# Row selection in attention plus mixture-of-depths: chosen rows fetched from DRAM instead of gathered by matmuls

## The chip, the cores and the metric

The kernel runs on one core of a Trainium2 chip. The metric is device time in microseconds (us) for one execution, the median of three runs. A profiled execution has its own time and, inside it, a span from the first to the last recorded instruction.

Engines are named as in the profile: PE (TensorE matmuls), PEld (its weight loads), DVE (VectorE), ACT (ScalarE), POOL (GpSimd), and SPq (SyncE's queue, which here only issues DMAs). Each engine runs its own instructions in program order, and waits between engines and DMAs go through semaphores that the framework places from the data dependences of the program as written.

## The reference

Inputs q, k, v have the shape (batch 8, heads 12, sequence 448, head size 64). The first half is cosine attention, the second a mixture-of-depths layer that changes only 128 chosen rows of each batch:

```
q_n = q / (norm(q) + 1e-6);  k_n = k / (norm(k) + 1e-6)
attn = softmax(q_n @ k_n^T / tau)
x    = (attn @ v) as (8, 448, 768)

scores = x @ w_gate
out    = x.copy()
for b in range(8):
    top = the 128 rows of batch b with the highest scores
    h   = relu(x[b, top] @ w1)                # 768 -> 1024
    g   = sigmoid(scores[b, top])
    out[b, top] = x[b, top] + g * (h @ w2)    # 1024 -> 768
```

## The kernel before

**Slots.** Two heads of one batch make a pair; there are N = 48 pairs, six to a batch (HP = 6). The main loop (L609) has one slot for each pair i: scores for pair i on PE, their exponentials on ACT, then the product with V for pair i-1 (`pv`, L309), its division into `x_tiles[b]` on DVE (`pv_evac`, L325), the transposes of q and k for pair i+1 (L251), and normalisation of pair i+2 on POOL (`scale`, L222). After `scale`, POOL converts V and (L349) the fresh 128 columns of x to bf16 (`half_x`, tile `xh`).

**Hooks.** The mixture-of-depths work of batch b is hung into later slots by a table: `at(slot, where, fn, ...)` appends a call to a list and `run(slot, where)` plays that list at a fixed place of the slot. The places, in program order within a slot, are D0 and D1 (early), P1b, then pv, A (right after pv_evac, before the slot's last scores), P2 (on POOL after `scale`, `values` and `half_x`), C, D3, and B (the slot's end). Calls at the same place run in the order in which they were appended. With s = 6(b+1), the first slot after batch b, the usual plan `late` (L531) is:

- store_x (L343) at s, place P2: two SPq DMAs that write the batch's x to `out`;
- gate at s+2 to s+5 (DVE); rank_prep at s+5 (POOL); rank_rep at s+5 B (PE); rank_count and pick at s+6 (DVE): `sel`, a one-hot 0/1 matrix of the chosen rows;
- select (L428) at s+7 A: eight small matmuls that give row indices and gate values, then DVE reductions; select_b on ACT;
- gather (L463) at s+7 B and s+8 A: 24 matmuls of `xh` against `sel` that give the chosen rows, already transposed, in PSUM; DVE copies them to `xeT`;
- ffn1 and ffn2 (L480, L509) in four parts at s+8 B to s+11 A: 48 and 16 matmuls;
- scatter (L514) at s+12 P2: an indirect DMA from POOL that adds the 128 result rows to those in `out` (compute_op=add).

The plans `mid`, `early` and `last` (L533 to L537) pull this forward for the last batches, so that two parts of ffn1 are evacuated by ACT there. All parts share the single PSUM bank `m_ps`.

**Order through DRAM.** scatter names the whole of `out_flat` as its target, since its rows are known only at run time. So a store_x later in the program waits for an earlier scatter to land, and a scatter waits for every earlier store.

**SPq** issues all loads of q, k and v (every third slot, L612, four groups ahead) and all stores, in program order.

**The end.** Batch 6 has its gather at slot 47 and its feed-forward after the loop. For batch 7, `gate` over the first 640 columns and four stores (two to `out`, two to a DRAM copy `x_copy`) stand at slot 47 P2; the last 128 columns (`x_last`) follow after the loop: two stores to `out`, two to `x_copy`. Then POOL issues scatter(6) (L704), an indirect fetch of batch 7's chosen rows from `x_copy` (L711), and, after two DVE operations that add them to the feed-forward result (L723), a plain last scatter (L726).

**Weights.** w1 and w2 are loaded with a cast by POOL at slots 7 and 10, P2 (L568, L569).

Of the kernel before, what the change touches and what calls it, by code (L numbers as in the profile page):

```python
# [17 lines left out]
def kernel(  # L18
# [18 lines left out]
    P = 128  # L37
# [115 lines left out]
    tokc = const.tile([P, NS, 2], BF16)  # L153
    for half in range(2):
        for col, base, step, mult in ((0, 0, 0, 4), (1, NC * half, 1, 3)):
            nc.gpsimd.iota(tokc[half * T:half * T + T, :, col], pattern=[[step, NS]],
                           base=base, channel_multiplier=mult,
                           allow_small_or_imprecise_dtypes=True)
# [150 lines left out]
    def pv(i):  # L309
        ex = exp_tiles[i]  # L310
        vo = vo_bufs[i % NB]
        for u in range(2):
            for j in range(NS):
                for c in range(NC):
                    nc.tensor.matmul(out=o_ps[:, u, j * E:(j + 1) * E],  # L315
                                     lhsT=ex[:, 2 * c + u, qc(j)],
                                     rhs=vo[:, u * NS + c], start=False,
                                     stop=(c == NC - 1), skip_group_check=True)
# [30 lines left out]
    def half_x(i):  # L349
        b, hp = divmod(i, HP)  # L350
        if hp == 0:
            xh_tiles[b] = xp.tile([P, NS, D], BF16, name="xh", bufs=3)
# [14 lines left out]
    def rank_prep(b, eng=nc.gpsimd):  # L367
        g = gates[b % 2]
        sg = moe.tile([P, NS, 3], BF16, name="sg")
# [58 lines left out]
    def select(b):  # L428
        sel, sg = st[b]["sel"], st[b]["sg"]
        pk = bank()  # L430
        for o, w, src in ((0, 2, tokc), (2, 3, sg)):
            for j in range(NS):
                nc.tensor.matmul(out=pk[:, o:o + w], lhsT=sel[:, j], rhs=src[:, j],
                                 start=(j == 0), stop=(j == NS - 1))
        gr = moe.tile([P, 1], FP32, name="gr")
        nc.vector.tensor_reduce(gr, pk[:, 2:5], axis=AX.X, op=ALU.add)  # L436
# [3 lines left out]
        nc.vector.tensor_scalar_add(idx, pks, float(b * S))  # L440
        st[b].update(idx=idx, gr=gr)
# [36 lines left out]


# [23 lines left out]

    def ffn2_evac(b, n, ps, eng):
        if n == 0:
            st[b]["oe"] = moe.tile([P, D], FP32, name="oe")
# [7 lines left out]
    def scatter(b):  # L514
# [3 lines left out]
            in_=st[b]["oe"][:CAP], in_offset=None, compute_op=ALU.add)  # L518
# [7 lines left out]
    def run(slot, where):  # L526
        for fn, args in work.pop((slot, where), []):
# [3 lines left out]
    late = dict(gate=((2, "D1"), (3, "D1"), (4, "D1"), (5, "D1")), rep=5, rank=6, select=7,  # L531
                ffn=((8, "B"), (9, "B"), (10, "B"), (11, "A")))
    mid = dict(late, ffn=((8, "B"), (9, "AA"), (9, "B"), (10, "A")))  # L533
    early = dict(gate=((2, "D1"), (3, "D1"), (3, "D1"), (4, "D1")), rep=4, rank=5,
                 select=6, ffn=((7, "B"), (8, "AA"), (8, "B"), (9, "A")))
    last = dict(gate=((1, "D1"), (2, "D1"), (2, "D1"), (3, "D1")), rep=3, rank=4,
                select=5, ffn=())  # L537
    for b in range(B - 1):
        s = HP * (b + 1)
        m = last if b == B - 2 else early if b == B - 3 else mid if b == B - 4 else late  # L540
        at(s, "P2", store_x, b)
        for j in range(NS):
            d, w = m["gate"][j]
            at(s + d, w, gate, b, j)
        at(s + m["gate"][3][0], "P1b", rank_prep, b)
        at(s + m["rep"], "B", rank_rep, b)
# [6 lines left out]
        at(s + m["select"], "B", gather, b, 0, "A" if b == B - 2 else "D")  # L553
        if b < B - 2:
            at(s + m["select"] + 1, "A", gather, b, 1)
        for (d, w), (fn, n) in zip(m["ffn"], ((ffn1, 0), (ffn1, 1), (ffn2, 0), (ffn2, 1))):
            at(s + d, w[0], fn, b, n, "A" if w == "AA" else "D")
            if fn is ffn2 and n == 1:
                at(s + d + 1, "P2", scatter, b)
    bb = B - 1  # L560
    gc = const.tile([P, NS], FP32)

    for j in range(NS):
        at(N - 1, "P2", gate, bb, j, 0, 5 * P, None, gc)
    at(N - 1, "P2", store_x, bb, None, 0, 5 * P)
    at(N - 1, "P2", store_x, bb, None, 0, 5 * P, x_copy)
    at(5, "D1", load_wg)
    at(7, "P2", load_w, w1_sb, moe_w1, kn[:, 1, 0, 0:1])  # L568
    at(10, "P2", load_w, w2_sb, moe_w2, kn[:, 1, 0, 0:1])  # L569
# [39 lines left out]
    for i in range(N + 1):  # L609
# [61 lines left out]
        if i < 3:  # L671
            warm(8)
        run(i, "B")
# [6 lines left out]
    pv_tails(N - 1)  # L680
    pv(N - 1)
    pv_evac(N - 1)
    gather(b, 1, "A", True)
    store_x(bb, x_last, 5 * P, D)
# [16 lines left out]
    for j in range(NS):  # L701
        rank_count(bb, j)
        pick(bb, j, nc.gpsimd if j < NC else nc.vector)
    scatter(b)  # L704
# [5 lines left out]
    xs = moe.tile([P, D], FP32, name="xs", bufs=1)  # L710
    nc.gpsimd.indirect_dma_start(  # L711
        out=xs[:CAP], out_offset=None, in_=x_copy[:, :],
        in_offset=bass.IndirectOffsetOnAxis(ap=st[bb]["row"][:CAP, 0:1], axis=0))
# [6 lines left out]
    oe = moe.tile([P, D], FP32, name="oe")  # L720
    for n in range(2):
        c = slice(n * ND, (n + 1) * ND)
        nc.vector.scalar_tensor_tensor(out=oe[:, c], in0=ps[n][:, :ND],  # L723
                                       scalar=st[bb]["gr"], in1=xs[:, c], op0=ALU.mult,
                                       op1=ALU.add)
    nc.gpsimd.indirect_dma_start(  # L726
        out=out_flat[:, :],
        out_offset=bass.IndirectOffsetOnAxis(ap=st[bb]["idx"][:CAP, 0:1], axis=0),
        in_=oe[:CAP], in_offset=None)
# [34 lines left out]
```

## Time and profile before

| what | value |
|---|---|
| median of three runs | 271.24 us (269.73 to 271.52) |
| profiled execution, its time | 268.42 us |
| its span | 266.6 us |
| around the span | 1.8 us |
| slots 17 to 34, mean length of six slots (one batch) | 29.1 us |
| end of the last scores to end of the span | about 28.5 us |

The slot lengths are read from the starts of the DVE copy qkT (L263), which occurs once in each slot. In the tables of the profile a group is a line of code, an engine and an operation, with its count, its busy time and the mean duration of one; "idle before" is the time that the engine stood still just ahead of it, with what ended that idle time. A DMA's "landing" runs from its issue to its completion, and its issuing instruction on POOL or SPq shows only the time to generate it. Busy time of PE counts overlapping matmuls, so its share is not a share of peak.

### The profile page before, as it was taken

What the parts mean: (1) busy time and instruction counts of PE and PEld (TensorE: products, weight loads), DVE (VectorE), ACT (ScalarE), POOL (GpSimd) and SP (SyncE); (2) the same over time, 40 slices, a digit from 0 to 9 for tenths busy, and PEclk for the clock granted to TensorE, in tenths of its full rate; (3) what the DMA queues carried; (4) which work ended last, traced back from release to release, by engine and by line L of the source; (5) the groups of instructions that cost most, each with busy time, mean ns of one, the idle gap of its engine ahead of it and who ended that gap; (6) DMA issues with size and microseconds to landing.
All of it is one profiled execution on the core that took longest, in us unless ns stands there. A gap on an engine that the chain in (4) does not pass through costs nothing.

```text
span 266.6 us, 10588 instructions
## 1 busy us (share of the span) xinstructions
PE 225.2 (84%) x4584; PEld 169.9 (64%) x4584; DVE 175.2 (66%) x472; ACT 203.3 (76%) x322; POOL 168.3 (63%) x234
## 2 busy tenths in 40 slices
PE   7678877586899979999899979998999899989920
PEld 6456655465678557767677757866786667757810
DVE  2424445474977778858877778678876976898401
ACT  3698999897897798888888789779878986683400
POOL 5367676979766568575966667757846885743131
PEclk9999999999999999999999999999999999999995
DMA  7999999999999974799679985999580049047861
GB/s 248 285 286 279 264 254 275 368 260 259 267 285 350 235 161 64 167 276 285 130 153 262 260 203 84 216 283 274 101 192 20 2 61 210 4 61 161 255 116 63
DMA packets 32431, 53.18 MB, mean 199 GB/s; under 512 B 2176, under 2 KB 28672, under 8 KB 31488
## 3 DMA queue, kind: packets, MB, share of 16 engines
q1 hardware_dynamic: 28976, 45.13, 63.9%
q0 software_dynamic: 2992, 6.69, 14.6%
q8 instruction: 36, 0.59, 1.0%
q10 hardware_dynamic: 416, 0.69, 0.7%
q14 instruction: 11, 0.09, 0.1%
HBM read 40.11 MB, written 15.53 MB: 209 GB/s over the span
## 4 chain that ended last, share of the span: by engine, by line
PE 35%; DMA 21%; DVE 16%; ACT 12%; issue 7%; SPq 4%; POOL 3%; POOLq 1%; ACTq 0%
DMA v_raw<-in_v_dram 11%; PE m_ps L491 7%; ACT expS L288 7%; PE m_ps L500 6%; PE sc L275 6%; PE o_ps L315 5%; DVE junk L416 4%; DVE junk L361 3%; DMA qk_raw<-in_k_dram 3%; DMA qk_raw<-in_q_dram 3%; PE sc L194 3%; ACT expS L291 3%; PE qkT_ps L257 3%; DVE xeT L457 2%; DVE x_b L333 2%
## 5 line engine op out<-in xcount | busy, mean ns | idle before, releaser
L288 ACT ACTIVATE expS<-sc 128x896 bf16<-128x896 f32 x144 | 125.3, 917 | 17.0 <-PE sc L275 16.4
L230 POOL TENSOR_TENSOR qkn<-qk_raw,rs 128x896 bf16<-128x896 f32 (+1 forms) x48 | 80.3, 1673 | 36.4 <-PE qkT_ps L257 26.3
L275 PE MATMUL sc<-qkT 64*128 64x448 bf16 x288 | 52.3, 358 | 14.8 <-DVE qkT L263 7.3
L187 ACT ACTIVATE sq<-qk_raw 128x896 bf16<-128x896 f32 x48 | 45.2, 947 | 2.1 <-DMA qk_raw<-in_k_dram 2.0
L315 PE MATMUL o_ps<-vo,expS 128*128 128x65 bf16 x1152 | 44.6, 193 | 1.5 <-issue 1.5
L315 PEld LDWEIGHTS <-expS 128*128 128x128 bf16 x1152 | 40.3, 97 | 2.1 <-issue 1.7
L275 PEld LDWEIGHTS <-qkT 64*128 64x128 bf16 x288 | 15.4, 92 | 37.3 <-issue 21.0
L263 DVE COPY qkT<-qkT_ps 128x960 bf16<-128x960 bf16 x48 | 31.3, 653 | 7.8 <-PE qkT_ps L257 6.8
L291 ACT ACTIVATE expS<-sc 128x448 bf16<-128x448 f32 x48 | 25.7, 536 | 13.3 <-PE sc L280 13.2
L333 DVE TENSOR_TENSOR x_b<-o_ps,rden 128x512 f32<-128x512 f32 x47 | 32.5, 691 | 1.6
L257 PEld LDWEIGHTS <-qkn 64*64 64x64 bf16 x1344 | 24.9, 109 | 12.9 <-issue 8.4
L257 PE MATMUL qkT_ps<-iden_b,qkn 64*64 64x64 bf16 x1344 | 30.4, 194 | 3.2 <-POOL qkn L230 2.1
L354 POOL CAST xh<-x_b 128x512 bf16<-128x512 f32 x47 | 29.7, 633 | 2.0 <-DVE gr L436 1.3
L361 DVE CUSTOM_DVE_ANT_0 junk<-x_b,wg_b 128x768 bf16<-128x768 f32 (+1 forms) x32 | 30.5, 953 | 0.5 <-DMA wg_b<-in_moe_w_gate_dram 0.3
L194 PE MATMUL sc<-sq,iden_b 128*128 128x112 bf16 x384 | 26.9, 215 | 2.4 <-ACT expS L288 2.3
L202 DVE TENSOR_REDUCE ss<-sc 128x14 f32<-128x112 f32 x48 | 12.8, 273 | 24.4 <-PE sc L194 24.0
L237 POOL CAST vo<-v_raw 128x448 bf16<-128x448 f32 x48 | 26.8, 557 | 0.8 <-DMA v_raw<-in_v_dram 0.7
L217 POOL TENSOR_SCALAR rs<-rs 128x28 f32<-128x28 f32 (+1 forms) x26 | 8.0, 307 | 25.8 <-ACT rs L211 21.7
L491 PEld LDWEIGHTS <-w_sb 128*128 128x128 bf16 x384 | 22.2, 98 | 3.3 <-issue 3.1
L194 PEld LDWEIGHTS <-iden_b 128*128 128x128 bf16 x384 | 20.8, 98 | 4.6 <-issue 1.7
L416 DVE SCALAR_TENSOR_TENSOR junk<-m_ps,own,tie 128x448 bf16<-128x448 f32 (+1 forms) x28 | 19.0, 678 | 0.5
L491 PE MATMUL m_ps<-xeT,w_sb 128*128 128x128 bf16 x288 | 18.1, 219 | 1.3 <-DVE xeT L457 1.3
(90 smaller groups left out, 275.6 us busy)
## 6 DMA issues: line engine op xcount, KB each, us to landing
qk_raw<-in_q_dram SPq DMA_DIRECT2D x15, 672.0 KB, 10.1
qk_raw<-in_k_dram SPq DMA_DIRECT2D x15, 672.0 KB, 12.0
v_raw<-in_v_dram SPq DMA_DIRECT2D x30, 192.0 KB, 9.6
out_dram<-x_b SPq DMA_DIRECT2D x7, 768.0 KB, 7.8
v_raw<-in_v_dram SPq DMA_DIRECT2D x30, 144.0 KB, 9.0
out_dram<-x_b SPq DMA_DIRECT2D x7, 576.0 KB, 4.7
w_sb<-in_moe_w_dram POOLq DMA_DIRECT2D x2, 1536.0 KB, 18.9
out_dram<-x_b SPq DMA_DIRECT2D x1, 640.0 KB, 6.7
```

The source lines that it names most:

```text
L187: nc.scalar.activation(sq_tiles[p], raw[gi % NRAW][0][:, :, g].rearrange("p a b d -> p a (b d)"), AF.Square)
L194: nc.tensor.matmul(out=dst, lhsT=iden_b, rhs=sq[:, :, s * D8:(s + 1) * D8], start=(s == 0), stop=(s == Dh // D8 - 1))
L230: eng.tensor_mul(kn[:, :, b0:b1], qk[:, :, g, b0:b1], rs[:, m, :, b0:b1].rearrange("p a (b o) -> p a b o", o=1) .to_broadcast([P, 2, b1 - ...
L257: nc.tensor.transpose(out=qkT_ps[r, o:o + T], in_=kn[r, a, s], identity=iden_b[r, r], tile_position=(u * T, u * T))
L263: nc.vector.tensor_copy(qkT_tiles[p], qkT_ps[:, :W])
L275: nc.tensor.matmul(out=sc[:, u, :S], lhsT=qkT[r, KO + c * P:KO + (c + 1) * P], rhs=qkT[r, :S], start=True, stop=True, tile_position=(u * D ...
L288: nc.scalar.activation(ex[:, 2 * c:2 * c + 2], sc[:, :, :S], AF.Exp, scale=inv_tau)
L291: nc.scalar.activation(ex[:, TAIL], sc[:, 0, :S], AF.Exp, scale=inv_tau)
L315: nc.tensor.matmul(out=o_ps[:, u, j * E:(j + 1) * E], lhsT=ex[:, 2 * c + u, qc(j)], rhs=vo[:, u * NS + c], start=False, stop=(c == NC - 1) ...
L333: nc.vector.tensor_mul(dst.rearrange("p j (u d) -> p j u d", u=2), o[:, :, :, :Dh], rden.to_broadcast([P, NS, 2, Dh]))
L361: nc.vector.tensor_tensor_reduce(out=junk[:, d0:d1], in0=src, in1=wg_b[:, d0:d1], scale=1.0, scalar=0.0 if prev is None else prev[:, j:j + 1],
L491: nc.tensor.matmul(out=ps[:, f * CAP:(f + 1) * CAP], lhsT=w1_sb[:, t, fc * P:(fc + 1) * P], rhs=xeT[t], start=(m == 0) if cut else (t == 0 ...
```

## The change

For batches 0 to 5 the rows are no longer gathered on PE. A new `fetch` reads the 128 chosen fp32 rows of x back from `out`, where store_x put them, by an indirect DMA from POOL; `half_xs` converts them to bf16 on POOL; `turn` transposes them by six PE transposes, and DVE copies the result. Those batches no longer convert x with `half_x`. The result is added to the fetched rows on DVE (in `ffn2_evac`, in place in `xs`), so their scatter is a plain write.

The places change too: store_x moves from s to s+3 for most batches, the fetch comes at the slot of select, half_xs one slot ahead of turn, and the four feed-forward parts move some slots later; ACT no longer evacuates any part inside the loop. The last batch's x is stored pair by pair at slots 43 to 47, to `x_copy` and to `out`. One of its four gate reductions is split into a POOL multiply and an ACT sum. The first part of the last pair's pv moves into slot 47. After the loop the fetch of batch 7 is issued ahead of scatter(6). In `select`, index and gate columns share one table `gtok`, so four matmuls do what eight did, and the index is reduced before the gate. The weight loads move to slots 8 and 14.

```diff
-    tokc = const.tile([P, NS, 2], BF16)
+    gtok = [const.tile([P, NS, 5], BF16, name=f"gtok{n}") for n in range(2)]
...
     def half_x(i):
         b, hp = divmod(i, HP)
+        if b < B - 2:
+            return
...
     def rank_prep(b, eng=nc.gpsimd):
-        sg = moe.tile([P, NS, 3], BF16, name="sg")
+        sg = gtok[b % 2][:, :, 2:]
...
     def select(b):
-        for o, w, src in ((0, 2, tokc), (2, 3, sg)):
-            for j in range(NS):
-                nc.tensor.matmul(out=pk[:, o:o + w], lhsT=sel[:, j], rhs=src[:, j],
-                                 start=(j == 0), stop=(j == NS - 1))
+        for j in range(NS):
+            nc.tensor.matmul(out=pk[:, :5], lhsT=sel[:, j], rhs=gtok[b % 2][:, j],
+                             start=(j == 0), stop=(j == NS - 1))
...
+    def fetch(b):
+        xs = moe.tile([P, D], FP32, name="xs")
+        st[b]["xs"] = xs
+        last = b == B - 1
+        nc.gpsimd.indirect_dma_start(
+            out=xs[:CAP], out_offset=None, in_=x_copy[:, :] if last else out_flat[:(b + 1) * S, :],
+            in_offset=bass.IndirectOffsetOnAxis(
+                ap=st[b]["row" if last else "idx"][:CAP, 0:1], axis=0))
+
+    def half_xs(b):
+        st[b]["xe"] = moe.tile([P, D], BF16, name="xe", bufs=1)
+        nc.gpsimd.tensor_copy(st[b]["xe"], st[b]["xs"])
+
+    def turn(b):
+        ps = bank().bitcast(BF16)
+        xe, xeT = st[b]["xe"], moe.tile([P, KD, CAP], BF16, name="xeT")
+        for t in range(KD):
+            nc.tensor.transpose(out=ps[:, t * CAP:(t + 1) * CAP],
+                                in_=xe[:, t * P:(t + 1) * P], identity=iden_b)
+        nc.vector.tensor_copy(xeT.rearrange("p t c -> p (t c)"), ps[:, :KD * CAP])
+        st[b]["xeT"] = [xeT[:, t] for t in range(KD)]
...
     def ffn2_evac(b, n, ps, eng):
+        if "xs" in st[b]:
+            c = slice(n * ND, (n + 1) * ND)
+            xs = st[b]["oe"] = st[b]["xs"]
+            nc.vector.scalar_tensor_tensor(
+                out=xs[:, c], in0=ps[:, :ND], scalar=st[b]["gr"], in1=xs[:, c],
+                op0=ALU.mult, op1=ALU.add)
+            return
...
     def scatter(b):
...
-            in_=st[b]["oe"][:CAP], in_offset=None, compute_op=ALU.add)
+            in_=st[b]["oe"][:CAP], in_offset=None,
+            **({} if "xs" in st[b] else dict(compute_op=ALU.add)))
...
+    late = dict(gate=(2, 3, 4, 5), rep=5, rank=6, select=7, turn=10, store=3,
+                ffn=("10B", "13B", "14B", "15A"))
+    plans = {b: late for b in range(B - 5)}
+    plans[B - 5] = dict(late, ffn=("10A", "12B", "13B", "14A"))
+    plans[B - 4] = dict(gate=(2, 3, 3, 4), rep=4, rank=5, select=6, turn=9, store=3,
+                        ffn=("9A", "11B", "12B", "13A"))
+    plans[B - 3] = dict(gate=(1, 2, 2, 3), rep=3, rank=4, select=5, turn=8, store=3,
+                        ffn=("8A", "8B", "9A", "11A"))
+    plans[B - 2] = dict(gate=(1, 2, 2, 3), rep=3, rank=4, select=5, store=0, ffn=())
...
+        if b == B - 2:
+            at(s + m["select"], "B", gather, b, 0, "A")
+        else:
+            at(s + m["select"], "P2", fetch, b)
+            at(s + m["turn"] - 1, "P2", half_xs, b)
+            at(s + m["turn"], "A", turn, b)
...
+    def gate_mul():
+        nc.gpsimd.tensor_mul(xg5, x_tiles[bb][:, NC, :5 * P], wg_b[:, :5 * P])
...
+    at(N - 1, "P2", gate_mul)
+    for hp in range(HP - 1):
+        for dst in (x_copy, None):
+            at(N - HP + 1 + hp, "P2", lambda d0=hp * P, dst=dst: store_x(
+                bb, x_tiles[bb][:, :, d0:d0 + P], d0, d0 + P, dst))
...
+            if fn is ffn2 and n == 1:
+                at(s + d + (place_ == "B"), "P2", scatter, b)
...
+        at(HP * (b + 1) + plans[b]["store"], "P2", store_x, b)
...
-    for j in range(NS):
+    for j in range(NC):
         at(N - 1, "P2", gate, bb, j, 0, 5 * P, None, gc)
-    at(N - 1, "P2", store_x, bb, None, 0, 5 * P)
-    at(N - 1, "P2", store_x, bb, None, 0, 5 * P, x_copy)
-    at(7, "P2", load_w, w1_sb, moe_w1, kn[:, 1, 0, 0:1])
-    at(10, "P2", load_w, w2_sb, moe_w2, kn[:, 1, 0, 0:1])
+    at(8, "P2", load_w, w1_sb, moe_w1, kn[:, 1, 0, 0:1])
+    at(14, "P2", load_w, w2_sb, moe_w2, kn[:, 1, 0, 0:1])
...
+        if not nxt:
+            pv_tails(i)
+            pv(i, (0,))
         run(i, "B")
...
-    pv_tails(N - 1)
-    pv(N - 1)
+    pv(N - 1, (1, 2))
     pv_evac(N - 1)
     gather(b, 1, "A", True)
+    xgs5 = moe.tile([P, 5 * P], FP32, name="xgs5", bufs=1)
+    nc.scalar.activation(xgs5, xg5, AF.Copy, accum_out=gc[:, NC:])
...
-    scatter(b)
     gather(bb, 0, "A", True)
...
+    fetch(bb)
+    scatter(b)
```

## The prediction

> **What bounds the kernel now.** I read the totals, then stretches of the loop, then the waits of the DMA queue, then the last 30 us in order of time. First the totals, and the busy time of one batch's 29 us, of the last slots and of the end:
>
> ```profile
> PE 225.2 (84%) x4584; PEld 169.9 (64%) x4584; DVE 175.2 (66%) x472; ACT 203.3 (76%) x322; POOL 168.3 (63%) x234
> ...
> 109.00:138.00 29.00, 27.42 (x575) 20.83 (x572) 22.17 (x58) 24.39 (x39) 20.38 (x28) 1.00 0.87 212
> ...
> 221.00:242.00 21.00, 19.86 (x390) 14.67 (x388) 18.08 (x48) 13.97 (x21) 10.13 (x15) 1.00 0.42 84
> 242.00:266.60 24.60, 12.44 (x145) 9.51 (x142) 7.64 (x26) 4.85 (x11) 6.71 (x11) 0.84 0.64 158
> ```
>
> Columns are length, PE, PEld, DVE, ACT and POOL busy, clock, DMA share, GB/s. In the middle PE is busy 27.4 of 29.0 us, ACT 24.4. PE sets the pace, and ACT is only 3 us below it: a slot relieved of PE work soon meets ACT. In the last 24.6 us PE is half idle, so a chain of waits rules there. The groups that the change touches:
>
> ```profile
> L473 PE MATMUL m_ps<-sel,xh 128*128 128x128 bf16 x160 | 11.1, 219 | 0.0
> L354 POOL CAST xh<-x_b 128x512 bf16<-128x512 f32 x47 | 29.7, 633 | 2.0 <-DVE gr L436 1.3 <-DVE x_b L333 0.8
> L457 DVE CAST xeT<-m_ps 128x512 bf16<-128x512 f32 x6 | 4.0, 672 | 0.0
> L457 DVE CAST xeT<-m_ps 128x256 bf16<-128x256 f32 x6 | 2.5, 412 | 0.0
> L515 POOL DMA_INDIRECT out_dram<-oe,idx x7 | 11.4, 1633 | 7.3 <-DMA x_copy<-x_last 6.3 <-issue 1.0
> ```
>
> Next SPq's own waits, then the end in order of time (start, duration):
>
> ```profile
> SPq L346 <- DMA out_dram<-oe,idx: 94.5, 6, 24.9
> ```
>
> ```profile
> 234.72 1.61 POOL L515 DMA_INDIRECT out_dram<-oe,idx  x1 [0.16 <-issue]
> ...
> 240.42 0.62 SPq L346 DMA_DIRECT2D out_dram<-x_b  x1
> ...
> 250.11 0.14 DVE L444 CAST row<-pks 128x1 int32<-128x1 f32 x1
> ...
> 253.78 1.60 POOL L515 DMA_INDIRECT out_dram<-oe,idx  x1 [6.30 <-DMA x_copy<-x_last]
> 256.14 1.02 POOL L711 DMA_INDIRECT xs<-x_copy,row  x1 [0.76 <-issue]
> 260.87 1.14 DVE L723 SCALAR_TENSOR_TENSOR oe<-w_ps,gr,xs 128x384 f32<-128x384 f32 x2 [7.65 <-DMA xs<-x_copy,row]
> 262.28 1.01 POOL L726 DMA_INDIRECT out_dram<-oe,idx  x1 [5.12 <-DVE oe L723]
> ```
>
> The reader should see two things. First, scatters and stores to `out` do wait for one another: scatter(5), issued at 234.72, lands 5.6 us later (the median for these), at 240.3, and the store behind it goes out at 240.42 although its x was ready at 237.5. Second, the row index of batch 7 is ready at 250.25, but its fetch goes out only at 256.14, because scatter(6) ahead of it on POOL waits for the last stores. PE has finished the last feed-forward at 255.1; the fetch lands at 260.7 and the rest follows.
>
> **What the Trainium skill says.** "DMA: Bandwidth & Descriptors", section "Two DMAs through the same engine are not ordered": the issuing engine has to wait for the first DMA's completion before a dependent one. The 94.5 us above are that wait. Section "Anatomy of one DMA — SWDGE (gpsimd) path" gives about 2.0 us plus bytes over 436 GB/s; for 128 rows of 3 KB my estimate from it is 2.9 us. This trace has 4.6 for the fetch and 5.6 for the adding scatter; I use the trace. "TensorE: Matmul & The Clock Gate", section "Part 4: PE-mode transpose", gives about 275 ns for a 128x128 bf16 transpose among other work. Here 28 transposes of 64x64 take 0.63 us together, so back to back they pipeline; the page's price is my upper bound only.
>
> **The body of the loop, batches 0 to 5.** PE loses the gather: 16 matmuls from 131.97 to 132.97 and 8 from 134.52 to 134.99, 1.47 us. It gains six transposes: at the gather's pace of 62 ns 0.37 us, at the page's price 1.65. I take 0.4. select drops four of eight matmuls that take 0.51 us in the chain, so 0.25. Net 1.3 us a batch, 7.9 us for six (0 at the page's price). What counts is what slots let through. The six slot lengths of a steady batch are 5.97, 4.70, 4.87, 4.77, 4.67, 4.28. The 4.28 slot carries 24 matmuls of ffn1 (1.5 us), so a slot with one ffn part costs about 4.4; the 5.97 slot carries both parts of ffn2. After: two slots with one ffn1 part each (4.4), one with both parts of ffn2 (5.97), one with rank_rep (4.7), one with select (4.87 - 0.25, led by DVE's rank_count), one with only turn (4.3, close to ACT's 4.1 a slot). Sum 28.4 against 29.3 (this batch, slots 18 to 23): **0.75 us a batch kept, 4.5 us in all** (ends 0 and 7.9).
>
> On other engines: DVE loses 0.67 + 0.41 and gains one copy of 768 bf16 columns, 0.53 at the pace of L263 (653 ns for 960); the new multiply-add takes 0.61 (L723) like the multiply before it. The two ffn1 evacuations taken from ACT (0.60 each) cost DVE 0.69 each, beside PE work. POOL loses 36 casts of 0.63 (22.8 us) and 0.6 a scatter (1.6 against 1.0 for the plain L726), and gains six fetches of 1.0 and six casts of 768 columns, 0.93 scaled from L354; POOL does not lead, so I count nothing. A fetch's 4.6 to 6 us are covered by the two slots (9.4 us) until half_xs. The 2.4 MB that the fetches read are 12 us of DMA at 200 GB/s, but the DMA share is 0.87; the loads run four groups ahead. Without that cover each fetch would add up to 2 us.
>
> Weights: w2's issue at slot 10 holds POOL (0.92 + 0.99) ahead of rank_prep(0), and PE stands 1.2 us for it (64.9). At slot 14 nothing so urgent is behind it: 0.5 us gained (0 to 1.2). First use of w2 is at slot 20, 27 us later, against 18.9 to land.
>
> store_x moves three slots towards the reuse of its x tile (two buffers): scatter(b-2) starts some 3.4 us after its slot's copy qkT, lands 5.0 later, then the second store 0.7 and its 7.8 us to land: 16.9. DVE overwrites the tile about 17.2 to 18 us after, and fetch comes at 21.9. I count 0, with 0.5 to 1 us of slack.
>
> **The end.** Late: ffn2's second part for batch 5 moves from slot 45 to 47, a swap within the PE-led slots. At slot 47 POOL now has gate_mul (1.28 us between 0.45 for 128 columns and 1.69 for 896), then scatter(5), **which stands in program order behind the pair store to `out` of that slot.** In before's time: x ready 237.5, four SPq issues of 0.62 to 240.2, landing 3.1 to 4.3 after the last one's start: 243.3. With 0.8 us of POOL's own latency scatter(5) runs 244.0 to 245.0. Behind it on POOL is xg (0.45), behind that on ACT the gate sum and the evacuation of ffn1(6), and PE's rank_rep_last waits for the gate. Before, these matmuls end at 244.6; now at 246.9, 2.3 later. (Slot 43 has the same wait for scatter(4), 1.5 to 2 us of POOL; the next transposes are just on time, so 0.) One gate reduction less on DVE (0.9) is offset by batch 5's multiply-add (0.61) in that slot.
>
> From there: row at 252.6; fetch at once, landed 257.3; PE done 257.4; multiply-adds 258.7; scatter(6), 1.8 after the fetch, lands 260.1; last scatter 260.3 instead of 262.28. **The end gains 2.0 us**: 6 from the early fetch, less 2.3 for the late row, less what scatter(6) takes. Ends: a loss of 1 if the store lands as slowly as the big ones (6.7), a gain of 5.3 if scatter(5) does not wait.
>
> **Sum**: 4.5 + 0.5 + 2.0 = 7.0 us off the profiled 268.42, so 261.4. The median of the runs is 271.24, 2.8 above the profiled run; the same difference gives **264.2 us**.
>
> **Rivals.** *No wait at slot 47* (chance 0.20): if the tracking does not tie scatter(5) to that store, the end gains 5.3: 260.9. Against it: the 2.9 us wait in the other direction at 240.42.
> *The gain is eaten by ACT and DVE* (0.20): ACT's 24.4 of 29 speaks for it, and qkT waits seen as idle PE; then the body keeps 0 to 1 and the end 2: 267 to 270.
> *The stores land late: slower* (0.14). From slot 21 on each store goes out right behind a scatter, and DVE's pv_evac in slot s+7, then POOL's fetch, wait for it; behind them are every later x_b, and POOL's `scale`. At 8.6 us of landing (7.8 plus slack) this starts to cost; stores here have taken up to 14.4 us. Three batches (2, 3, 4) pay: at 14.4 some 5.8 each, 17 in all less some slack, about 276. It ends slower than before by over 1% from 11.8 us of landing on (9.7 us over three batches). For it: the DMA share of 0.87 and new fetch traffic; against: all steady stores took 7.7 to 7.8.
> My forecast has 0.46.
>
> **How the numbers follow.** Within 1% of 271.24 (268.5 to 274.0) is about what cannot be told from no change. Faster: 0.44 + 0.20 + 0.09 = 0.73; same: 0.02 + 0.11 + 0.02 = 0.15; slower 0.12. Range 257.5 (no wait and most of the 7.9) to 270.5 (gain eaten).
>
> **What would show it.** Right: a steady batch of 28.3 to 28.7 us; x_b without a DMA wait; scatter(5) preceded on POOL by a wait of 3 to 5 us for the x_b store; the last fetch issued within 1 us of its row, and the last scatter bound by scatter(6) or PE. Wrong: DVE's x_b or POOL's fetch waiting on a store; xs late for half_xs; ACT's exponentials back to back with PE idle; transposes near 275 ns each.

## The result, and the profile after

The changed kernel is **slower**: 282.75 us (median, 280.56 to 286.86) against 271.38 for the kernel before, ratio 1.039 [1.030, 1.049]. Its profiled execution took 280.56 us with a span of 278.5 (before: 268.42 and 266.6). The forecast was 264.2. Runs of one kernel differ by up to 4%, so medians here are of all runs, ratios with their 95% intervals of the faster ones alone, within some 1.5% of the fastest, and a ratio is not the quotient of two medians.

First the totals, then busy time in two steady batches (slots 17 to 28) and in the last slots (length, PE, PEld, DVE, ACT, POOL busy, clock, DMA share, GB/s), all of the changed kernel but the line from 87.84, which is the same two batches in the kernel before:

```profile
PE 225.5 (81%) x4444; PEld 166.6 (60%) x4444; DVE 173.5 (62%) x466; ACT 204.0 (73%) x322; POOL 161.3 (58%) x215
...
89.59:148.11 58.52, 52.13 (x1080) 38.37 (x1078) 42.90 (x114) 48.30 (x77) 36.72 (x44) 0.99 0.76 198
...
87.84:145.51 57.67, 53.87 (x1122) 40.37 (x1122) 44.32 (x117) 48.57 (x78) 39.63 (x53) 1.00 0.81 189
...
225.00:256.00 31.00, 25.07 (x411) 17.15 (x410) 20.83 (x49) 14.97 (x22) 15.43 (x19) 0.83 0.38 103
```

No engine has noticeably more to do than before, and none is fuller. PE, busy 53.87 of 57.67 us (93%) in these slots before, is at 89%, and in the last slots at 81% with a clock of 0.83. So PE waits. The groups of the new operations, then the longest new waits (total, times, longest), the last line being ACT's wait before:

```profile
L494 POOL CAST xe<-xs 128x768 bf16<-128x768 f32 x6 | 7.9, 1311 | 2.7 <-DMA xs<-out_dram,idx 2.7
L500 PE MATMUL m_ps<-iden_b,xe 128*128 128x128 bf16 x36 | 3.7, 250 | 10.3 <-POOL xe L494 10.3
```

```profile
ACT expS L293 <- PE sc L282: 35.7, 21, 7.6
...
PEld L500 <- POOL xe L494: 11.1, 6, 3.0
...
ACT expS L291 <- PE sc L280: 13.2, 16, 1.5
```

Read the second group's last field: PE stood idle 10.3 us in all, always for the cast on POOL, in front of six sets of six transposes; a set costs 0.5 us. ACT's wait for the fourth block of scores, which PE computes right behind the transposes, was 13.2 us before and is 35.7 now.

The end in order of time. The forecast's sequence is there, late. The first line names a gate as what POOL waited for, but the scatter reads no gate, and the last pair store, issued at 252.37, landed at 254.8; so I read the 3.37 us as the wait for that store:

```profile
255.64 1.29 POOL L550 DMA_INDIRECT out_dram<-xs,idx  x1 [3.37 <-DVE gc L366]
258.01 0.45 POOL L746 TENSOR_TENSOR xg<-x_last,wg_b 128x128 f32<-128x128 f32 x1 [1.08 <-DVE x_last L336]
...
266.07 1.04 POOL L487 DMA_INDIRECT xs<-x_copy,row  x1 [3.07 <-DVE row L448]
267.41 1.64 POOL L550 DMA_INDIRECT out_dram<-oe,idx  x1 [0.30 <-ACT hT L465]
273.96 1.00 POOL L550 DMA_INDIRECT out_dram<-xs,idx  x1 [4.91 <-DMA out_dram<-oe,idx]
```

**Where the time went** is seen in the start of each slot's copy of qkT on DVE, one mark per slot (us from the start of the profiled execution). A slot's length is its mark less the one before. Transposes of fetched rows stand in slots 16, 22, 28, 34, 39 and 44. The lower rows are experiments told of below; that of "cast early" took 279.27 us, where the kernel's fastest run took 274.03.

| kernel | slot 16 | 28 | 32 | 35 | 39 | 44 | 46 | span |
|---|---|---|---|---|---|---|---|---|
| before | 87.84 | 145.51 | 166.11 | 181.03 | 200.25 | 224.92 | 233.81 | 266.6 |
| after | 89.59 | 148.11 | 166.96 | 184.31 | 207.23 | 237.60 | 246.38 | 278.5 |
| cast early | 89.29 | 148.69 | 167.48 | 185.98 | 208.60 | 237.15 | 246.09 | 277.5 |
| cast early, ffn1 at B | 90.99 | 151.57 | 169.71 | 186.23 | 206.31 | 233.01 | 244.02 | 274.1 |
| cast on ACT | 87.60 | 145.53 | 163.82 | 181.74 | 204.19 | 232.43 | 241.22 | 273.0 |
| transposes at slot end | 86.22 | 142.43 | 161.02 | 178.01 | 200.69 | 230.81 | 241.56 | 273.8 |
| the same, short plans redone | 84.86 | 141.44 | 160.03 | 177.02 | 198.61 | 224.78 | 235.44 | 268.0 |

In the steady part, slots 17 to 28, the changed kernel takes 58.5 us and the kernel before 57.7: its two slots with transposes take 5.44 us each, and that uses up what the others gain. Most of the loss comes in the shortened plans of batches 3 to 5, where the first ffn1 part follows the transposes at once: slots 34, 39 and 44 take 7.44, 7.82 and 10.95 us where they took 4.28, 5.73 and 5.34, together 10.9 us more. Slot 16, the first with transposes, loses another 3.8 (8.12 for 4.28): its rows landed 10.6 us after the issue and POOL stood 2.7 us for them. So the six slots with transposes lose 17.0 us, and all the rest is 5.1 us shorter. PE's wait for the cast is 10.3 of the 17.0.

The worst slot, 44, in three views of the changed kernel. PE, POOL, then DVE in order of time:

```profile
227.78 1.09 PE L318 MATMUL o_ps<-vo,expS 128*128 128x65 bf16 x24
231.78 0.82 PE L500 MATMUL m_ps<-iden_b,xe 128*128 128x128 bf16 x6 [2.91 <-POOL xe L494]
233.25 2.72 PE L518 MATMUL m_ps<-xeT,w_sb 128*128 128x128 bf16 x24 [0.65 <-DVE xeT L502]
```

```profile
226.75 1.69 POOL L232 TENSOR_TENSOR qkn<-qk_raw,rs 128x896 bf16<-128x896 f32 x1 [1.78 <-PE qkT_ps L259]
228.38 1.28 POOL L239 CAST vo<-v_raw 128x448 bf16<-128x448 f32 x1
229.62 1.34 POOL L359 CAST xh<-x_b 128x512 bf16<-128x512 f32 x1
230.90 0.82 POOL L494 CAST xe<-xs 128x768 bf16<-128x768 f32 x1
```

```profile
227.37 1.88 DVE L366 CUSTOM_DVE_ANT_0 junk<-x_b,wg_b 128x768 bf16<-128x768 f32 x1
...
229.29 1.19 DVE L366 CUSTOM_DVE_ANT_0 junk<-x_b,wg_b 128x768 bf16<-128x768 f32 x1
```

The cast is last in a line on POOL, and that line starts late, because `scale` waits for PE's transposes of the slot before. And the line is slow: the `vo` cast takes 1.28 us where 0.56 is usual, `xh` 1.34 for 0.61, the gates 1.88 and 1.19 for 0.90. They take turns: the first gate ends 0.8 us after `scale` does, the `vo` cast 0.4 us after that gate, the second gate 0.8 after that cast, and so on. This is what the Trainium skill, "SBUF — State Buffer", section "SBUF: two separate sides", states: a DVE operation with two SBUF inputs and a POOL operation that reads SBUF need one pair of ports, which the first holds for its whole instruction. The trace agrees: each ends its own usual duration, less some 0.1 us, after the one before it. In a steady slot it is the cast itself that pays: 1.55 us, of which 0.82 is its own.

Then PE, idle for 2.9 us, loses its clock, within that wait already (the changed kernel, stretches around that gap):

```profile
220.00:228.90 8.90, 7.93 (x149) 5.17 (x143) 6.66 (x13) 6.58 (x11) 5.69 (x7) 1.00 0.73 230
228.90:231.80 2.90, 0.02 (x1) 0.03 (x2) 2.37 (x6) 0.00 (x0) 2.82 (x3) 0.76 0.29 73
231.80:237.00 5.20, 4.55 (x43) 3.55 (x45) 1.25 (x2) 0.63 (x2) 1.08 (x1) 0.50 0.36 120
```

At half clock 24 matmuls of ffn1 take 2.72 us instead of 1.50. The changed kernel's mean clock is 0.66 in 49 to 54, 86 to 91 and 250 to 255 us, and 0.57 in 230 to 238; in the kernel before it is 1.00 from 5 to 258. That is some 17 us at half clock, which by my estimate, had PE been busy throughout, would cost up to 8.5 us. This part is not separated from the waits by any run.

### The profile page after: what moved, and what is told of

Its sections match the earlier page's. It is cut to its first block, busy times and chain, and to the rows that moved or that the text cites. A ratio compares the mean times of both kernels' runs of the same rounds, so it can differ in the third digit from the quotient of the medians.

```text
span 278.5 us, 10317 instructions
## 1 busy us (share of the span) xinstructions
PE 225.5 (81%) x4444; PEld 166.6 (60%) x4444; DVE 173.5 (62%) x466; ACT 204.0 (73%) x322; POOL 161.3 (58%) x215
## 4 chain that ended last, share of the span: by engine, by line
PE 45%; DVE 13%; ACT 13%; DMA 9%; issue 8%; POOL 7%; SPq 3%; POOLq 1%; ACTq 0%
PE sc L277 8%; ACT expS L290 7%; PE m_ps L518 6%; PE m_ps L527 6%; PE o_ps L318 5%; PE qkT_ps L259 5%; PE sc L196 4%; DVE junk L421 4%; DMA qk_raw<-in_k_dram 3%; DMA v_raw<-in_v_dram 3%; PE sc L282 3%; POOL xe L494 2%; ACT expS L293 2%; DMA out_dram<-oe,idx 2%; DVE qkT L265 2%
## 5 line engine op out<-in xcount | busy, mean ns | idle before, releaser
L277 PE MATMUL sc<-qkT 64*128 64x448 bf16 x288 | 53.7, 368 | 19.0 <-DVE qkT L265 9.5
L293 ACT ACTIVATE expS<-sc 128x448 bf16<-128x448 f32 x48 | 25.8, 537 | 36.0 <-PE sc L282 35.7
L318 PE MATMUL o_ps<-vo,expS 128*128 128x65 bf16 x1152 | 45.3, 194 | 1.6 <-issue 1.6
L259 PEld LDWEIGHTS <-qkn 64*64 64x64 bf16 x1344 | 25.7, 111 | 12.8 <-issue 9.7
L259 PE MATMUL qkT_ps<-iden_b,qkn 64*64 64x64 bf16 x1344 | 31.2, 197 | 2.6 <-POOL qkn L232 2.1
L239 POOL CAST vo<-v_raw 128x448 bf16<-128x448 f32 x48 | 27.4, 571 | 2.4 <-DMA v_raw<-in_v_dram 2.4
L518 PEld LDWEIGHTS <-w_sb 128*128 128x128 bf16 x384 | 23.4, 102 | 5.4 <-issue 4.6
L518 PE MATMUL m_ps<-xeT,w_sb 128*128 128x128 bf16 x288 | 19.7, 228 | 2.6 <-DVE xeT L502 1.9
L527 PE MATMUL m_ps<-w_sb,hT 128*128 128x384 bf16 x96 | 18.5, 338 | 1.1 <-DVE gr L444 1.1
```

The source lines that it names most:

```text
L259: nc.tensor.transpose(out=qkT_ps[r, o:o + T], in_=kn[r, a, s], identity=iden_b[r, r], tile_position=(u * T, u * T))
L277: nc.tensor.matmul(out=sc[:, u, :S], lhsT=qkT[r, KO + c * P:KO + (c + 1) * P], rhs=qkT[r, :S], start=True, stop=True, tile_position=(u * D ...
L293: nc.scalar.activation(ex[:, TAIL], sc[:, 0, :S], AF.Exp, scale=inv_tau)
L318: nc.tensor.matmul(out=o_ps[:, u, j * E:(j + 1) * E], lhsT=ex[:, 2 * c + u, qc(j)], rhs=vo[:, u * NS + c], start=False, stop=(c == NC - 1) ...
L518: nc.tensor.matmul(out=ps[:, f * CAP:(f + 1) * CAP], lhsT=w1_sb[:, t, fc * P:(fc + 1) * P], rhs=xeT[t], start=(m == 0) if cut else (t == 0 ...
L527: nc.tensor.matmul(out=ps[:, :ND], lhsT=hT[t], rhs=w2_sb[:, t, n * ND:(n + 1) * ND], start=(t == 0), stop=(t == KF - 1))
```

## The experiments

Kernels were compared on one chip at a time with the kernel before, whose medians there were 271.15 us (cast early, cast twice, weights back, new end alone), 269.69 (the one with the merged select, and the three with ffn1 at B), 272.38 (the four from the transposes at slot end to the cast on ACT), 268.99 (short plans redone, two kernels) and 268.57 (the last).

**Cast early.** Only the cast moves, ahead by most of a slot:

```
-            at(s + m["turn"] - 1, "P2", half_xs, b)
+            at(s + m["turn"] - 1, "P1b", half_xs, b)
```

> The changed kernel with one call moved: half_xs goes from P2 to P1b of the same slot, ahead of scale on POOL, where POOL stood idle 2 to 4 us waiting for the transposes. Theory 1 (PE stalls at turn because the cast stands behind scale and values on POOL, and a stalled PE holds up the scores and so ACT): the six waits of turn for xe (10.3 us) go below 1 us, the slots that carry turn fall from 5.4 to 11 us to 4.3 to 6, and the time falls by 10 to 14 us, to 269 to 273. Theory 2 (the reordered feed-forward plan for the last batches is what costs, the cast only shows it): the waits go, but slots 33 to 45 stay long and the time falls by less than 6 us. Theory 3 (late data: the fetch, not the cast, is what xe waits for): the wait moves from PE to POOL, qkn comes late, and the time stays within 3 us of 282.7.

Measured: 279.41 us, from runs of 274.03, 279.27, 279.54 and 281.32, too far apart for a ratio; the trace is of the second, span 277.5. In it PE's wait for the cast fell from 10.3 to 2.4 us and the cast's mean duration from 1.31 to 0.83, and the span only by 1.0. Its other waits:

```profile
POOL xe L494 <- DMA xs<-out_dram,idx: 12.8, 3, 4.7
PE m_ps L518 <- DVE xeT L502: 7.9, 5, 2.6
```

A slot earlier the rows have not always landed, and POOL stands for them. And where ffn1 follows in the slot, PE now waits for the copy `xeT`, which stands on DVE behind the gates and pv_evac. The expectation named the right wait, and in this run two others stand in series with it. Whether the run of 274.03 us, close to theory 1, had them is not on record.

**The cast twice.** The cast, unmoved, is executed two times:

> The changed kernel with the cast of the fetched rows done twice in a row (same result). Theory 1: each of six turns waits some 1.5 us more, so the time rises by 8 to 11 us, to 291 to 294. Theory 2 or 3: POOL has slack or waits for data anyway, and the time rises by less than 3 us.

Measured: 287.75 us, ratio 1.063 [1.052, 1.075]; PE's wait for `xe` is 16.0 us, up 5.7, and the time up 5.0 against the changed kernel. The rise is below the 8 us of theory 1 and above the 3 of the others, but the added wait comes out at the end nearly whole: it is on the path. The added cast costs some 0.9 us each time and not 1.5, because by then DVE's gate is over.

**Cast early, weights back** at slots 7 and 10 of the kernel before:

> e1 with the weight loads back at slots 7 and 10. In the changed kernel the first fetch lands 10.6 us after its issue, beside w2's load of slot 14, and the slot with turn(0) takes 8.1 us. Theory 1 with this as a second cause: the first fetch lands in 4 to 6 us and the time falls 1 to 3 us below e1. If the loads' place does not matter: within 1 us of e1.

Measured: 278.32 us, ratio 1.022 [1.011, 1.032]. POOL's waits for the rows halve (6.2 us), the time is 1.1 below the cast moved alone, inside their spread. The first fetch lands after 8.5 us instead of the changed kernel's 10.6, not after the 4 to 6 expected, so the load's place is no large part.

**The new end alone**, on the kernel before (stores pair by pair, the gate product on POOL, fetch ahead of scatter(6), pv split):

> The kernel before with only the end of the change: pair stores of the last batch, the split gate reduction, part of pv moved into slot 47, and the fetch of batch 7 ahead of scatter(6). Gather, scatters with add, feed-forward plan and weight loads stay as before. In the changed kernel the stretch after x_last is 3.6 us shorter and slot 47 is 3.0 us longer, which I put down to the feed-forward part moved there. If so, this kernel keeps the 3.6 without the 3.0: 3 to 4 us below before, 267 to 268.5. If the stores' waits cost slot 47, it ends within 1.5 us of before.

Measured: 266.68 us, ratio 0.983 [0.973, 0.994]; but the profiled span is 266.8, no less than before, and **with the merged select added** and 20 runs it is this:

> The kernel before with the end of the change (e3) and with the merged select of four matmuls, index before gate; gather, scatters with add, feed-forward plan and weight loads as before. PE loses 0.25 us a batch in slots led by DVE's rank_count, so I expect 0 to 1.5 us below e3, 265 to 267.

Measured: 269.59 us, ratio 0.998 [0.993, 1.003]. No gain. Two conflicts could take it. The trace of the end alone shows scatter(5) waiting 3.2 us for the pair store, and the gate product on POOL against a gate on DVE, 3.40 us where its neighbour takes 0.82:

```profile
238.74 0.82 DVE L362 CUSTOM_DVE_ANT_0 junk<-x_b,wg_b 128x640 bf16<-128x640 f32 x1
...
239.60 3.40 DVE L362 CUSTOM_DVE_ANT_0 junk<-x_b,wg_b 128x640 bf16<-128x640 f32 x1
...
243.23 0.69 DVE L334 TENSOR_TENSOR x_last<-o_ps,rden 128x512 f32<-128x512 f32 x1
```

x_last is 1.5 us later than the 241.70 of the kernel before. But the early copy alone, below, has neither conflict and shows no gain in its runs either, so that they took it is not shown.

**Cast early, and the first ffn1 part at B** in batches 3 to 5 ("10A" to "10B", "9A" to "9B", "8A" to "8B"):

> e1 (cast at P1b) with the first ffn1 part of batches 3, 4 and 5 moved from place A, right behind turn, to place B at the end of the same slot. In e1 the waits for xe are gone, but PE now waits 7.9 us for xeT, whose copy stands on DVE behind the gate reductions and pv_evac, and in slots 34, 39 and 44 the PE clock then falls to half. Theory 1, widened (two waits in series, cast on POOL and copy on DVE, each followed by work that PE must do in order): with both covered PE waits for neither, slots 34, 39 and 44 fall from 8.2, 7.0 and 9.1 to 5 to 6 us, and the time falls to 269 to 272. Theory 2 (the late plan holds too much work for its slots): those slots stay above 7 and the time stays within 3 us of e1's 279.

Measured: 275.83 us, ratio 1.020 [1.012, 1.029]. Slots 34, 39 and 44 fall to 4.10, 4.60 and 5.06 us. Part of this only moved behind the mark: slots 35, 40 and 45 rise to 5.99, 5.98 and 7.58, from 3.77, 3.77 and 5.36. POOL now waits 15.4 us for rows.

**Only ffn1 at B**, the cast as in the change:

> The changed kernel (cast at P2, as it was) with only the first ffn1 parts of batches 3, 4 and 5 moved to place B: the fourth corner of the square of cast early or late and ffn1 at A or B. Theory 1, widened: PE still waits some 10 us for xe, but no longer for xeT as well; 275 to 279. If the cast alone matters it stays at 282 to 284; if the place of ffn1 alone matters it comes down to where e4 is.

Measured: 281.74 us, ratio 1.041 [1.033, 1.049]: nothing, against the changed kernel's 1.039, where both together gave 1.020. PE still waits 9.7 us for the cast. So the place is worth nothing until that wait has gone. What the cast alone is worth can't be read from runs of 274 to 281 us.

**The two with ffn2 of batch 5 out of slot 47** ("11A" to "9B"):

> e4 with the second ffn2 part of batch 5 at slot 45 place B instead of slot 47 place A. In the changed kernel slot 47 waits 1.1 us for the single PSUM bank between select and this part and runs 1.4 us of it ahead of the last scores; x_last comes 10.9 us after the copy of slot 46 against 7.9 before. If that explains the 3.0 us lost there: 2.5 to 3.5 us below e4. If the work only moves: within 1 us of e4.

Measured: 276.36 us, ratio 1.019 [1.011, 1.028]. x_last comes 6.7 us after the mark of slot 46 instead of 8.9, but slot 46 takes 5.60 us instead of 3.43: work moved, no gain.

**Transposes at slot end.** The cast stays two slots after the fetch; the transposes move half a slot, and ffn1 with them:

```
-            at(s + m["turn"], "A", turn, b)
+            at(s + m["turn"], "B", turn, b)
...
-                ffn=("10B", "13B", "14B", "15A"))
+                ffn=("11A", "13B", "14B", "15A"))
```

In batches 3 to 5 the first parts went to "11B", "10B" and "9A", and in batch 5 the next two to "9B" and "10B".

> The changed kernel with the six transposes at the end of their slot, after the scores, in place of its middle; the cast stays where the changed kernel has it (two slots after the fetch, so that the fetch keeps its time), and the first ffn1 part comes half a slot later. Theory (TensorE stands in its order behind a cast that is itself held behind the scale and the values on POOL and behind DVE's gates; neither the fetch nor the transposes are too dear): the cast's 1.2 us of waiting in the steady batches and up to 6 in the short plans are covered by some 2.5 us of other matmuls, no wait for xe and none for the fetch is left, and the time falls from 282 to 268-273, at or just below the kernel before, whose six-slot batch is 29.3 us; a steady batch falls to 27.9-28.3. Rival A (the fetch is too late in itself, or its transfers disturb the others): POOL waits as before for xs and the time stays near 276. Rival B (DVE, which copies xeT and does the two combining evictions, has become the bound): the wait moves to xeT and rank counting at the end of the slot, with 276 to 280.

Measured: 276.75 us, ratio 1.027 [0.998, 1.056]. The time is rival A's, but its reason is not: POOL waits 1.4 us for rows, PE 1.9 for the cast. In the table this kernel stands 5.1 us **ahead** of the kernel before at slot 32. Slots 17 to 28 of this kernel:

```profile
86.22:142.43 56.21, 51.26 (x1080) 38.45 (x1079) 43.43 (x115) 48.66 (x78) 36.91 (x44) 1.00 0.85 218
```

That is 0.73 us a batch less than before (57.67 for both), close to what the forecast kept (0.75), though in another plan than the one forecast. From slot 32 on it loses 12.8, in part through a fault of my replan that PE's order of time shows (slot 35 of this kernel):

```profile
177.90 0.36 PE L277 MATMUL sc<-qkT 64*128 64x448 bf16 x2
180.06 2.72 PE L518 MATMUL m_ps<-xeT,w_sb 128*128 128x128 bf16 x24 [1.79 <-DVE junk L421]
```

ffn1 sits in the slot in which DVE counts ranks from the only bank `m_ps`, so PE waits for the bank, and runs at a clock of 0.51 after it (180 to 183 us).

**The early copy of x alone**, on the kernel before: x_copy pair by pair and the fetch ahead of scatter(6); the stores to `out` and all four gates as they were.

> The kernel before with two edits of the end only: the copy of the last batch's x goes out pair by pair from slot 43 on (the stores of the result stay where they are, behind the scatter of batch 5), and the last fetch is issued ahead of the scatter of batch 6. Neither the gate product on POOL nor the early stores of the result are taken over, the two parts that took back the gain when the whole end was tried alone. Theory (the end is worth something if these two conflicts are left out): x_last stays at 241.7 us and the row at 250.3 in the profiled execution; the fetch, issued at 256.1 before, is issued at 250.5-251.5, the scatter of batch 6 follows and lands by 258, and the last scatter is issued at 257.5-259 in place of 262.3: 3-5 us less, ratio 0.982-0.989. Rival (the end hangs on the scatter of batch 6 as soon as it follows the fetch): the last scatter waits for it until 261 or later, and the gain is below 1.5 us.

Measured: 267.72 us over 20 runs, ratio 0.998 [0.993, 1.003]; span 264.3.

```profile
252.29 1.08 POOL L712 DMA_INDIRECT xs<-x_copy,row  x1 [5.02 <-issue]
253.68 1.59 POOL L515 DMA_INDIRECT out_dram<-oe,idx  x1 [0.30 <-issue]
259.96 1.01 POOL L728 DMA_INDIRECT out_dram<-oe,idx  x1 [4.69 <-DMA out_dram<-oe,idx]
```

The fetch goes out 3.9 us earlier, the last scatter only 2.3, because it now waits for scatter(6). The runs don't show even these 2.3. And the fetch leaves 2.2 us after its row (249.91 + 0.14); the last kernel below settles why. **Both together:**

> Both together: the changed kernel with the transposes at the end of their slot, and in the end only the early copies of x and the fetch ahead of the scatter of batch 6 (all four gate parts on DVE and the stores of the result behind the scatter of batch 5, as in the kernel before). Theory: the gains lie one after the other on the path and add: the time of the run with the transposes at slot end minus 1-4 us, 264-270, ratio 0.975-0.995 to the kernel before. Rival (slot 47 or the scatter of batch 5, now late, gives the gain back): no more than 1 us from the run with the transposes at slot end.

Measured: 281.01 us, ratio 1.049 [1.037, 1.060], above both expectations; span 275.4. At slot 46 its trace is 2.3 us ahead of the run with the transposes at slot end (239.31 against 241.56), and behind it 3.9 us are lost: 2.4 until x_last (a gate more on DVE, 0.8, and ffn2 at reduced clock, 2.47 us for 1.46), the rest where the last fetch again leaves 2.2 us after its row. This explains the profiled run; not all of the median's distance.

**The cast on ACT** (`nc.scalar.activation(..., AF.Copy)` in place of POOL's copy):

> The changed kernel with the cast of the fetched rows on ACT in place of POOL, at the same place of the program. Theory (on POOL the cast stands behind scale and values, and takes 1.55 us in place of 0.82 because POOL and DVE lock each other out of SBUF): on ACT it stands behind the third expS alone and has a constant duration of about 0.9-1.0 us; TensorE's wait for xe falls from 10-11 us to below 4; ACT has 1 us more to do in seven slots and waits for the fetch where that is late (some 1-3 us in all); where ffn1 follows at once, the wait for xeT takes its place, as when the cast was moved early. Time 276-279. Rival (it is the turn's place in TensorE's order alone, whoever casts): the wait for xe stays above 8 us and the time at 280-284. Rival (ACT is close to the bound, so that a cast there delays expS): the score wait of ACT goes down, its busy time is on the path, and the time is 282-287.

Measured: 275.33 us, ratio 1.020 [0.994, 1.046]. The waits of this kernel:

```profile
PE m_ps L518 <- DVE xeT L502: 6.0, 3, 2.6
ACT xe L494 <- DMA xs<-out_dram,idx: 3.5, 1, 3.5
...
PE m_ps L500 <- ACT xe L494: 3.0, 1, 3.0
```

At the same place of the program, off POOL, each cast takes 0.85 us and PE's wait falls from 10.3 to 3.0 us in one turn, the one whose rows were late. So POOL's line and the shared ports made the wait, not the turn's place alone. The steady slots 22 and 28 fall from 5.44 to 4.34 and 4.33 us, what the forecast gave them. But slots 34, 39 and 44 still take 7.05, 7.29 and 9.06: there PE now waits 1.5, 1.9 and 2.6 us for `xeT`. That is the series of waits, and most of the short plans' loss stays. The interval of the ratio is wide; the trace is the evidence here, not the time.

**The short plans redone.** The run with the transposes at slot end, with batches 3 to 5 as ("12B", "13B", "14A", "14B"), ("11B", "12B", "13A", "13B") and ("9A", "9B", "11A"), the last part of ffn2(5) and scatter(5) after the loop:

> The run with the transposes at slot end, replanned for the last three batches alone: no part of ffn1 or ffn2 in a slot whose PSUM bank is held by the rank counting of the next batch (batch 3: slots 36B, 37B, 38A, 38B; batch 4: 41B, 42B, 43A, 43B; batch 5: 45A, 45B, 47A, and its last part in the end, behind the gates of x_last, with its scatter ahead of the last gather). In the run before this one the steady part stood 5.1 us ahead of the kernel before at slot 32 and lost 12.8 us from there to slot 46, mostly in four slots of 7.2 to 7.9 us in which ffn1 waited 1.8 us for DVE's rank counting to free the one bank. Theory (places alone: the one bank and the in-order queues took the gain, not the fetch): these four slots fall to about 5, the copy of qkT in slot 46 is at 232-237 in place of 241.6 (233.8 in the kernel before), the end is within 1 us of the changed kernel's, and the time is 262-269, ratio 0.97-0.995. Rival (the short plans have too much of everything, DVE and POOL included, so that the waits only move, as when ffn2 of batch 5 was moved): the loss after slot 33 stays above 8 us and the time at 273-278.

**And with the early copy:**

> The same with the end that has only the early copies of x and the fetch ahead of the scatter of batch 6. Theory: 1-3 us below the run it is built on, which is what this end showed alone (span 264.3 against 266.6). Rival (the scatter of batch 5, now in the end, lands after the stores of the result and holds the scatter of batch 6 and so the last one): 1-4 us above it.

Measured: 273.43 us, ratio 1.020 [1.015, 1.025], span 268.0, and 272.62 us, 1.013 [1.006, 1.020], span 269.6. Both stay above the kernel before. Of the slots named, 36, 40 and 41 fell from 7.94, 7.16 and 7.91 to 4.43, 4.73 and 4.94 us, and slot 33 kept its 7.38. Slot 46's mark, 235.44, is the theory's; the time, 273.43, is the rival's. The loss after slot 32 is 7.7 us instead of 12.8. So the places explain 5.1 us of it. What the other 7.7 are, full queues in the short plans for one, was not shown.

**The copy of x_last first.** The kernel with the early copy alone, and the stores of batch 7 to `out` moved behind the copy of x_last:

```
-    at(N - 1, "P2", store_x, bb, None, 0, 5 * P)
...
-    store_x(bb, x_last, 5 * P, D)
     store_x(bb, x_last, 5 * P, D, x_copy)
+    store_x(bb, None, 0, 5 * P)
+    store_x(bb, x_last, 5 * P, D)
```

> The kernel with the early copy of x alone, with one more edit: the stores of batch 7 to the result (640 columns and x_last) are issued behind the copy of x_last, no longer ahead of it. In the run with the early copy the last fetch left 2.2 us after its row, with no releaser shown, at about the time at which the copy of x_last landed (issued at 248.72, 3.2 us); this copy stood behind six other stores on SP. Theory (the fetch waits for the landing of that copy): the copy is issued at 242.5-244 and the fetch leaves within 0.6 us of the row, at 250.3-250.8; scatter of batch 6 at 251.8-252.4, last scatter at 258-258.7 in place of 262.28 in the kernel before and 259.96 in that run; 3.5-4 us below the kernel before, ratio 0.984-0.990. Rival (the delay is POOL's own, or the result's stores, now later, hold the scatter of batch 6 until they land): the fetch or the last scatter stays within 0.5 us of that run, ratio 0.993-1.003.

Measured: 265.98 us, ratio **0.986 [0.978, 0.994]**, from six runs: an interval below 1, as the new end alone had from four, which 20 runs of it with the merged select did not bear out. Here the trace has the mechanism; how much of it the time keeps is open. The row is ready at 252.80 + 0.14 in its profiled run, of 267.53 us, whose marks were 2.7 us late by slot 46 already, 2.4 of them by slot 35, ahead of all that was edited:

```profile
253.23 1.08 POOL L712 DMA_INDIRECT xs<-x_copy,row  x1 [3.07 <-DMA out_dram<-x_b]
255.19 1.59 POOL L515 DMA_INDIRECT out_dram<-oe,idx  x1 [0.89 <-issue]
261.31 1.01 POOL L728 DMA_INDIRECT out_dram<-oe,idx  x1 [4.53 <-DMA out_dram<-oe,idx]
```

The first line names a store to `out`, but the fetch reads only x_copy. It follows its row by 0.3 us instead of 2.2, and from row to last scatter it is 8.5 us, against 10.1 with the early copy alone and 12.2 in the kernel before. So the fetch had waited for a small copy that stood on SP behind six larger or less urgent stores. What this end gives, it gives without any of the fetches in the loop.

## Why the prediction was wrong

- **The failed step** is in "On other engines": six casts of "0.93 scaled from L354; POOL does not lead, so I count nothing". PE itself waits for this cast, at place A of the slot after the one in which it is issued. It took 1.55 us in four of six turns, stood behind `scale` and `values`, and PE waited 10.3 us for it. With the cast executed twice the wait rose by 5.7 us and the ratio from 1.039 to 1.063; with the cast on ACT the wait fell to 3.0, though the ratio, 1.020 [0.994, 1.046], is too wide to price that. I added up POOL's busy time and never asked which of its operations PE would reach first.
- "one with only turn (4.3)": 5.44 us in steady batches. The difference is the 1.2 us of PE's wait there; with the cast on ACT it is 4.3. The PE arithmetic held: six transposes take 0.51 us (0.4 forecast), and with the transposes at slot end, where hardly anything waits for the cast, PE's busy time in slots 17 to 28 is 51.26 us against 53.87 before, 1.3 a batch as forecast, of which 0.73 was kept. The forecast's two sums, 29.3 and 28.4, differ by 0.9 and not 0.75; nothing hangs on it.
- The second step that failed is "0.75 us a batch kept, 4.5 us in all": the short plans were priced like steady batches. There ffn1 follows its transposes at once, so that cast, transposes, `xeT` and ffn1 are one chain across POOL, PE and DVE, and slots 34, 39 and 44 cost 10.9 us more. With the cast off POOL they still cost some 8 more. Even with the places redone 7.7 us are lost after slot 32, and that rest stays open.
- "A fetch's 4.6 to 6 us": 10.6, 7.7, 8.6, 8.3, 7.9 and 4.2. Its size was off, the cover nearly held: POOL waited 2.7 us, all at the first fetch.
- Weights: the 0.5 us to be gained is not seen, nor ruled out. Slot 10's mark is 0.75 us later, but it lies between 58.4 and 63.2 us in other runs, with either place of the loads.
- store_x: landing 7.7 us, no wait of x_b: right, and the "stores land late" rival did not happen. My only rival on the slow side had another mechanism.
- Slot 47 as "a swap": x_last came 10.9 us after slot 46's mark (7.9 before). ffn2 there waits 1.1 us for select to free the bank and then runs at reduced clock, 2.40 us for 1.47; taking it out of the slot only moved the time.
- The end: scatter(5) waited for the pair store 3.4 us, as forecast, and harmlessly, since x_last was later still. The fetch left 0.3 us after its row and scatter(6) set the last scatter: both right. From x_last to the span's end 24.9 us became 21.3, 3.6 less where 2.0 were forecast; with the 3.0 lost in slot 47, the end as a whole kept 0.7.

## What to carry to other kernels

When work moves from a full engine to an idle one, don't price the idle engine's busy time: find the operation that the full engine waits for, and read what stands ahead of it in its own queue and who shares its ports. Give such a handover half a slot of other matmuls, then look for the next wait in the chain, since several in series hide one another. Where one small transfer releases the last chain, issue it ahead of the large ones on its queue.

## What was not expected of the hardware

PE was idle for 2.9 us in slot 44 of the changed kernel, and the clock fell before that wait was over. PE's last matmul ended at 228.87; the mean clock is 1.00 from 228.9 to 230.3 and 0.50 from 230.5 to 231.8, so it fell some 1.5 us into the wait. With the transposes at slot end a wait of 1.8 us, in slot 35, was followed by a clock of 0.51. The Trainium skill, "TensorE: Matmul & The Clock Gate", section "Why this matters for your kernels", advises against gaps above some 3 us; here the clock fell in shorter ones. The wait of 2.9 us cost 1.2 us more in the next ffn1 alone.

The port conflict of DVE and POOL can cost several times the operation itself: 0.82 us became 3.40 for a gate beside two POOL operations (1.14 and 2.06 us; the new end alone).
